# One row of a weight matrix loaded to 32 partitions in six transfers around another matrix's rows, and 29 matrix products fewer, in a decode step bound by its loads

## The chip, the core and the metric

The kernel runs on one NeuronCore of one Trainium2 chip. A core has a matrix engine (TensorE, PE in the profile; its weight loads are shown as PEld), a vector engine (VectorE, DVE), a scalar engine (ScalarE, ACT), GpSimd (POOL) and SyncE (SP), and 16 DMA engines that bring data from HBM into the core's on-chip memory of 128 partitions. DMAs are issued from a queue of SP or ACT. The metric is the device time of one execution in microseconds (us); lower is better.

## The reference, cut to what matters

```python
# B = 2, D = 576, H = 32 heads, Sk = 4096, Dh = 128, F = 4608; all float32
g = sigmoid((x * gate_w).sum(-1, keepdims=True))
q = (x @ wq).reshape(B, 1, H, Dh).transpose(0, 2, 1, 3)
p = softmax(einsum("bhqd,bhkd->bhqk", q, k_cache) * Dh ** -0.5)
a = einsum("bhqk,bhkd->bhqd", p, v_cache).transpose(0, 2, 1, 3).reshape(B, 1, H * Dh) @ wo
b = gelu(x @ w1 + b1) @ w2 + b2
out = g * a + (1 - g) * b
```

One token for each of two sequences: attention over a cache of 4096 keys and values, and a dense layer pair beside it, mixed by a gate. Each weight and each cache entry is read once, 308.6 MB in all.

## The kernel before

**Loads.** All large loads go out on SP's queue in one fixed order: wq, w1, then 16 pairs of a tile of k_cache and a tile of v_cache (each tile is four heads of one sequence, 128 partitions x 16384 floats), then `LAST`: w2 and wo. They land in `ring`, which has three slots of 16384 floats in each partition. A slot is loaded again when the engine that reads it is done, so SP waits for that engine before it issues the load; SP works in order. Each DMA also has one of eight completion semaphores in turn, so it waits until the DMA eight places ahead of it has landed where that isn't known yet.

**w2 and wo as rows.** w2 has 4608 rows of 576; partition p holds its rows 36p to 36p+35, so "row r of w2" in the kernel is a slab of one row from each of the 128 partitions, 36 slabs in all (`NF`). wo is held in the same way as 32 slabs. The list `LAST` (line 66) groups the slabs into the last three ring slots and, within a slot, into transfers. In `load_last` (line 144) each entry is one DMA over 128 partitions, with two exceptions: 384 of the 576 columns of w2's row 35 are left out of the transfer of rows 28 to 35 and go as entry `wx` to 16 partitions, 8 pieces of 384 floats in each, by four DMAs of 4 partitions (line 156); and wo's row 31 goes in three parts (288, 144 and 144 columns).

**What is done with them.** `acc_mm` (line 364) multiplies one slab of w2 (with `hg`, the gated hidden layer) or of wo (with `oP`, the attention result) into the accumulator `acc`, as two products of 288 columns. `mlp_out(lo, hi)` does it for w2's slabs, `wo_out` for wo's, and `mlp_x` for the 384 columns in 16 partitions, with `hx`, a copy of the last column of `hg` spread over 16 partitions by eight small products (line 417). From wo's row `FOLD` = 23 on, `last_out` (line 449) uses another accumulator, `res`, with four products of 144 columns for each row (`part`). ACT meanwhile copies `acc` (line 452), and after row `FOLD` + 3 four products with `fold` add that copy into `res`. Then come the products of rows up to 31, four small copies, and the store of the result.

**The start.** x and gate_w are turned by ten small products (`xps`, line 271): four slabs for w1, the remainder as two, and four slabs again for wq, since the two matrices' rows lie on the partitions differently. Five products (line 280) form the gate's sum `zps`.

**Order of PE's work at the end** (lines 610 to 630): `mlp_out(0, 14)`, the last values tile, `mlp_out(14, 20)` around the attention result's normalisation, `mlp_out(20, 24)`, `mlp_x`, `mlp_out(24, 36)`, `wo_out(0, 23)`, `last_out`. PE works through its products in this order.

Of the kernel before, what the change touches and what calls it, by code (L numbers as in the profile page):

```python
# [12 lines left out]
P = 128  # L13
# [6 lines left out]
def kernel(  # L20
# [47 lines left out]
        (("w2", 28, 36), ("wx", 0, 1), ("wo", 0, 15)),  # L68
        (("wo", 15, 23), ("wo", 23, 27), ("wo", 27, 30), ("wo", 30, 31), ("wo", 31, 32)),
    )  # L70
    FOLD = 23
# [37 lines left out]
    def load_w(w, rows, c):  # L109
        if c < len(rows):  # L110
            n = rows[c] * w.shape[1]
            lo = sum(rows[:c]) * P
            src = w[lo:lo + rows[c] * P].rearrange("(p r) n -> p (r n)", r=rows[c])
        else:
            n = w.shape[1] // 2
            src = w[NX * P:].rearrange("q (e n) -> (q e) n", e=2)
# [18 lines left out]
    XE, XC, XW = 4, 4, 384  # L135
    XL = D - XW
    XP = XE * XC
    XS = P // XP
    srcx2 = w2.rearrange("(e c s r) n -> c r e s n", e=XE, c=XC, s=XS)[:, NF - 1, :, :, XL:]

    def length(w, a, z):
        return XS * XW if w == "wx" else (z - a) * D - (XW if (w, z) == ("w2", NF) else 0)

    def load_last(m):
# [5 lines left out]
        for w, a, z in LAST[m]:  # L150
            if w == "wx":
                xt = t[:XP, o:o + XS * XW]
                rows[w] = xt.rearrange("p (s n) -> p s n", s=XS)
                o += XS * XW
                for c in range(XC):
                    nc.sync.dma_start(xt[c::XC].rearrange("e (s n) -> e s n", s=XS), srcx2[c])
                continue
            if (w, z) == ("w2", NF):
                nc.sync.dma_start(t[:, o:o + length(w, a, z)], srcs[w][:, a * D:z * D - XW])
                for r in range(a, z):  # L160
                    rows[w, r] = t[:, o + (r - a) * D:o + min((r - a + 1) * D, length(w, a, z))]
# [101 lines left out]
    def x_rows(rows):  # L263
        ends = [sum(rows[:c]) * P for c in range(len(rows) + 1)]
        return [xg[:, lo + r:hi:n] for n, lo, hi in zip(rows, ends, ends[1:]) for r in range(n)]

    srcx = x_rows(ROWS["w1"]) + [xe[:, 0], xe[:, 1]] + x_rows(ROWS["wq"])
# [11 lines left out]
    for c in range(NX + 1):  # L279
        nc.tensor.matmul(zps, gT[:, c:c + 1].to_broadcast([P, P]), xT[:, c, :B], start=(c == 0), stop=(c == NX))  # L280
# [8 lines left out]
    def proj(w, ts, banks, width):  # L289
        full = NG * len(banks) * width  # L290
        for c, n in enumerate(ROWS[w] + (1,)):
            last = c == len(ROWS[w])
            for r in range(n):
                k = sum(ROWS[w][:c]) + r
                for m, ps in enumerate(banks):
                    for j in range(NG):
# [4 lines left out]
                        else:  # L301
                            o += r * full
                            lhs = xT[:, k if w == "w1" else NX + 2 + k]
# [112 lines left out]
    for s in range(XS):  # L416
        nc.tensor.matmul(
            hxps[:, s], ident.rearrange("p (q s) -> p s q", s=XS)[:, s], hg[:, NF - 1], start=True, stop=True
        )
# [239 lines left out]
```

## Time and profile before

| | |
|---|---|
| median of 3 runs | 721.73 us (721.68 to 721.9) |
| profiled execution, first to last instruction (span) | 719.7 us |
| median less span: what lies around the instructions | 2.0 us |
| busy: DVE, PE, POOL, ACT | 71%, 31%, 20%, 6% |
| DMA engines busy over the span, SP's queue | 99.2% |
| moved | 308.83 MB, 429 GB/s |

The profiled execution's own device time is not listed apart from its span; the span and the 2.0 us around it together are taken as the 721.73 us of the runs. "L371" is line 371 of the kernel before. In a product's row the count is twice that of the products, as each float32 product is two passes on PE. In a timeline, the time in square brackets is how long the engine sat idle ahead of the row, and what ended that. In rows of windows the columns are: stretch, its length, busy time and count of instructions of each engine, the granted clock of TensorE (1.00 is full), the share of the 16 DMA engines' time spent on packets, and GB/s.

### The profile page before, as it was taken

To read this page: it belongs to the slowest core of one execution; us is meant where nothing else is said; L and a number is where in the kernel's file an instruction comes from. 1 tells how busy PE (TensorE), PEld (TensorE's weight loads), DVE (VectorE), ACT (ScalarE), POOL (GpSimd) and SP (SyncE) were. 2 spreads that over 40 slices of the span, in tenths; PEclk is the share of its full clock that TensorE was granted. 3 is DMA by queue.
4 is the path that set the end of the run, shared out by engine and by line. 5 is a ranking of instruction groups with operands and counts; after the bars stand their busy time and mean duration, and the time that the engine had idled before them with its cause. 6 is when DMAs were issued, how large, how long until landed. Compare 5 with 4: busy or idle time off the path is not lost.

```text
span 719.7 us, 3913 instructions
## 1 busy us (share of the span) xinstructions
PE 223.4 (31%) x1663; PEld 66.1 (9%) x1663; DVE 512.0 (71%) x137; ACT 40.0 (6%) x156; POOL 145.0 (20%) x35
## 2 busy tenths in 40 slices
PE   0675022040514050404133140405060503214198
PEld 0321000010101010101000010101010100000024
DVE  0004969779695969596969879696959695988910
ACT  0110010100001010101010100001010101010000
POOL 2000130404050403022040404040403122040400
PEclk9967557565757575655756575757565665657588
DMA  9999999999999999999999999999999999999997
GB/s 408 412 443 434 426 444 419 455 416 455 416 444 428 426 441 430 438 430 444 430 434 426 441 430 437 431 433 437 437 434 441 423 431 437 430 441 431 420 424 308
DMA packets 7126, 308.83 MB, mean 429 GB/s; under 512 B 810, under 2 KB 1342, under 8 KB 1604
## 3 DMA queue, kind: packets, MB, share of 16 engines
q1 hardware_dynamic: 7060, 308.55, 99.2%
q8 instruction: 13, 0.21, 0.1%
q14 instruction: 5, 0.04, 0.0%
q10 hardware_dynamic: 48, 0.03, 0.0%
HBM read 308.57 MB, written 0.00 MB: 429 GB/s over the span
## 4 chain that ended last, share of the span: by engine, by line
DMA 45%; DVE 35%; PE 17%; ACT 1%; issue 1%; ACTq 0%; POOL 0%; DVEq 0%; POOLq 0%
DMA ring<-in_A_k_cache_dram 39%; DVE ring L512 19%; PE av L551 10%; DVE s L517 10%; DVE s L518 5%; DMA ring<-in_B_w_dram 4%; PE acc L371 3%; DMA ring<-in_gate_w_dram 3%; PE oall L568 2%; PE qps L304 1%; DVE avs L562 1%; PE res L463 0%; ACT p L537 0%; DVE m L522 0%; PE zps L280 0%
## 5 line engine op out<-in xcount | busy, mean ns | idle before, releaser
L512 DVE TENSOR_TENSOR ring<-ring,q 128x16384 f32<-128x16384 f32 x16 | 275.6, 17225 | 110.1 <-DMA ring<-in_A_k_cache_dram 110.1
L516 POOL TENSOR_TENSOR ring<-ring 128x3968 f32<-128x3968 f32 x16 | 137.0, 8565 | 491.3 <-DVE ring L512 491.3
L551 PE MATMUL av<-ring,p 128*32 128x512 f32 x1024 | 141.6, 715 | 167.6 <-ACT p L537 167.6
L517 DVE TENSOR_REDUCE s<-ring 128x66 f32<-128x8448 f32 x16 | 143.2, 8953 | 1.3
L568 PE MATMUL oall<-avs,pick 128*64 128x512 f32 x16 | 14.8, 1028 | 195.1 <-DVE avs L562 167.7
L518 DVE TENSOR_REDUCE s<-ring 128x62 f32<-128x3968 f32 x16 | 68.4, 4277 | 0.1
L551 PEld LDWEIGHTS av<-ring,p 128*32 128x32 f32 x1024 | 36.0, 129 | 278.8 <-issue 220.6
L537 ACT ACTIVATE p<-s,bs 32x128 f32<-32x128 f32 x64 | 25.5, 398 | 479.9 <-DVE bs L531 478.7
L352 PE MATMUL qb<-qm,spread 64*128 64x512 f32 x8 | 8.3, 1138 | 71.4 <-POOL qm L348 71.4
L395 DVE TENSOR_TENSOR ring<-hps,ring 128x384 f32<-128x384 f32 x3 | 1.7, 559 | 32.2 <-PE hps L304 32.0
L371 PE MATMUL acc<-ring,hg 128*2 128x288 f32 (+1 forms) x142 | 14.4, 561 | 25.3 <-DMA ring<-in_B_w_dram 25.3
L568 PEld LDWEIGHTS oall<-avs,pick 128*64 128x64 f32 x16 | 2.2, 196 | 201.9 <-DVE avs L562 201.9
L284 DVE TENSOR_SCALAR gb<-gb 128x2 f32<-128x2 f32 x1 | 0.2, 169 | 24.4 <-ACT gb L283 24.4
L483 DVE COPY ring<-res 2x144 f32<-2x144 f32 x1 | 0.3, 296 | 19.3 <-PE res L463 19.3
L304 PE MATMUL hps<-ring 128*32 128x384 f32 x120 | 12.8, 596 | 0.0
L562 DVE TENSOR_TENSOR avs<-av,selr 128x512 f32<-128x512 f32 x8 | 5.5, 682 | 10.1 <-PE av L551 10.1
L348 POOL TENSOR_TENSOR qm<-qall,mine 64x512 f32<-64x512 f32 x4 | 4.1, 1035 | 40.3 <-ACT qall L331 40.3
L537 ACT ACTIVATION_READ_ACCUMULATOR p<-s,bs 32x1 f32 x64 | 11.8, 184 | 0.0
L304 PE MATMUL qps<-ring 128*32 128x512 f32 x80 | 10.7, 697 | 0.0
L271 PE MATMUL xps<-ident,ring 3*128 3x3 f32 x10 | 1.5, 254 | 23.8 <-DMA ring<-in_gate_w_dram 22.8
L352 PEld LDWEIGHTS qb<-qm,spread 64*128 64x128 f32 x8 | 2.0, 308 | 74.5 <-POOL qm L348 74.5
L354 ACT COPY q<-qb 128x512 f32<-128x512 f32 x4 | 2.3, 585 | 106.3 <-PE qb L352 106.3
(88 smaller groups left out, 79.5 us busy)
## 6 DMA issues: line engine op xcount, KB each, us to landing
ring<-in_B_w_dram SPq DMA_DIRECT2D x2, 4608.0 KB, 34.3
ring<-in_B_w_dram SPq DMA_DIRECT2D x2, 4032.0 KB, 28.6
ring<-in_A_wo_dram SPq DMA_DIRECT2D x1, 4320.0 KB
ring<-in_A_wo_dram SPq DMA_DIRECT2D x1, 2304.0 KB, 22.4
ring<-in_B_w_dram SPq DMA_DIRECT2D x1, 2112.0 KB
ring<-in_B_w_dram SPq DMA_DIRECT2D x1, 1152.0 KB
ring<-in_A_wo_dram SPq DMA_DIRECT2D x1, 1152.0 KB
ring<-in_A_wq_dram SPq DMA_DIRECT2D x1, 1024.0 KB
```

The costliest lines, as they stand in the source:

```text
L304: nc.tensor.matmul(ps[32 * j:32 * j + 32, :width], lhs, ts[c][:, o:o + width], start=(k == 0), stop=last, skip_group_check=True,)
L348: nc.gpsimd.tensor_mul(t, qall.unsqueeze(1).to_broadcast([NO, NQ, DH]), mine[:, u[0]:u[-1] + 1].unsqueeze(2).to_broadcast([NO, NQ, DH]),)
L352: nc.tensor.matmul(ps, spread, t.rearrange("p u d -> p (u d)"), start=True, stop=True)
L371: nc.tensor.matmul(acc[o:o + m, u - s * DS:v - s * DS], lhsT, rhs[:, u - lo:v - lo], start=start, stop=stop, skip_group_check=True,)
L512: nc.vector.tensor_mul(kt[i], kt[i], qs[i].unsqueeze(1).to_broadcast([P, R, DH]))
L516: nc.gpsimd.tensor_add(t[:, :, :DH2], t[:, :, :DH2], t[:, :, DH2:])
L517: nc.vector.tensor_reduce(st[i][:, HALVED:], kt[i][:, HALVED:], AX.X, ALU.add)
L518: nc.vector.tensor_reduce(st[i][:, :HALVED], t[:, :, :DH2], AX.X, ALU.add)
L537: nc.scalar.activation(p[w, :, e * RB:(e + 1) * RB], st[i][w].rearrange("p (t c) -> p t c", c=RB), AF.Exp, bias=bias[i][w], accum_out=rs[w ...
L551: nc.tensor.matmul(ps[32 * j:32 * j + 32], p[:, 32 * t + EB * (1 - half):32 * t + EB * (1 - half) + 32], vt[i][:, RB * t:RB * (t + 1)].rea ...
L562: nc.vector.tensor_mul(t, avs[i].rearrange("p (r d) -> p r d", d=DH), selr.unsqueeze(2).to_broadcast([P, RB, DH]))
L568: nc.tensor.matmul(oall, pick[:, NO - G - i * G:2 * NO - G - i * G], avs[i].rearrange("p r d -> p (r d)"), start=(i == 0), stop=(i == N // ...
```

## The change

Six edits. (1) w2's rows 28 to 34 go to 128 partitions, and row 35 whole to partitions 0 to 31, four pieces of 576 floats in each, by six DMAs: three of 6 partitions ahead of wo's rows 0 to 14, two of 6 and one of 2 partitions behind them. (2) `mlp_x` is 8 products of 288 columns over 32 partitions, where it was 16 (half of them 96 columns wide) over 16 partitions; `mlp_out` no longer has row 35's remaining product of 192 columns; `hx` takes four products instead of eight. (3) `mlp_x` is done behind `wo_out(0, 15)`. (4) `FOLD` goes from 23 to 27, so rows 23 to 26 of wo take two products each instead of four, and the four fold products stand behind row 29 instead of row 26. (5) Both parts of w1 are laid out on the partitions as wq is, four rows to a partition, so x is turned by six products instead of ten; each partition still reads the same lengths in one piece. (6) `zps` is one product, with a multiplication and a sum on DVE ahead of it, instead of five products. Removed are 4 (transposes), 4 (`zps`), 4 (`hxps`), 8 (`mlp_x`), 1 (row 35) and 8 (rows 23 to 26): 29.

```diff
-        (("w2", 28, 36), ("wx", 0, 1), ("wo", 0, 15)),
+        (("w2", 28, 35), ("wx", 0, 3), ("wo", 0, 15), ("wx", 3, 6)),
...
-    FOLD = 23
+    FOLD = 27
...
-            lo = sum(rows[:c]) * P
-            src = w[lo:lo + rows[c] * P].rearrange("(p r) n -> p (r n)", r=rows[c])
+            lo = sum(rows[:c]) * w.shape[1]
+            src = w[:NX * P].rearrange("(p r) n -> p (r n)", r=NX)[:, lo:lo + n]
...
-    XE, XC, XW = 4, 4, 384
-    XL = D - XW
-    XP = XE * XC
+    XE, XP = 6, 32
     XS = P // XP
-    srcx2 = w2.rearrange("(e c s r) n -> c r e s n", e=XE, c=XC, s=XS)[:, NF - 1, :, :, XL:]
+    XT = 768
+    srcx2 = w2.rearrange("(s q r) n -> q s r n", q=XP, s=XS)[:, :, NF - 1]
...
             if w == "wx":
-                xt = t[:XP, o:o + XS * XW]
-                rows[w] = xt.rearrange("p (s n) -> p s n", s=XS)
-                o += XS * XW
-                for c in range(XC):
-                    nc.sync.dma_start(xt[c::XC].rearrange("e (s n) -> e s n", s=XS), srcx2[c])
-                continue
...
+                if a == 0:
+                    rows[w] = t[:XP, o:o + XS * XT].rearrange("p (s n) -> p s n", s=XS)[:, :, :D]
+                for c in range(a, z):
+                    u, v = c * XE, min((c + 1) * XE, XP)
+                    nc.sync.dma_start(rows[w][u:v], srcx2[u:v])
                 o += length(w, a, z)
                 continue
...
-    srcx = x_rows(ROWS["w1"]) + [xe[:, 0], xe[:, 1]] + x_rows(ROWS["wq"])
+    srcx = [xg[:, r:NX * P:NX] for r in range(NX)] + [xe[:, 0], xe[:, 1]]
...
-    for c in range(NX + 1):
-        nc.tensor.matmul(zps, gT[:, c:c + 1].to_broadcast([P, P]), xT[:, c, :B], start=(c == 0), stop=(c == NX))
+    xz = temp((NX + 1) * B).rearrange("p (b c) -> p b c", b=B)
+    nc.vector.tensor_mul(
+        xz, xT[:, :NX + 1, :B].rearrange("p c b -> p b c"), gT.unsqueeze(1).to_broadcast([P, B, NX + 1])
+    )
+    zs = temp(B)
+    nc.vector.tensor_reduce(zs, xz, AX.X, ALU.add)
+    nc.tensor.matmul(zps, ones.to_broadcast([P, P]), zs, start=True, stop=True)
...
     def mlp_x():
         for s in range(XS):
-            acc_mm(hx[:, s], rows["wx"][:, s], s, lo=XL)
+            acc_mm(hx[:, s], rows["wx"][:, s], s)
...
-            if r == FOLD + 3:
+            if r == FOLD + 2:
...
-    mlp_out(20, 24)
+    mlp_out(20, NF - 1)
+    wo_out(0, 15)
     mlp_x()
-    mlp_out(24, NF)
-    wo_out(0, FOLD)
+    wo_out(15, FOLD)
     last_out()
```

PE's last products stand like this in the kernel before, from the end of `mlp_x` (`hx`) through the last of w2's slabs (`hg`) and wo's (`oP`) to the two accumulators `acc` and `res`:

```order
L371 MATMUL acc<-ring,hx 2x96
L371 MATMUL acc<-ring,hx 2x288
L371 MATMUL acc<-ring,hg 2x288 x22
L371 MATMUL acc<-ring,hg 2x192
L371 MATMUL acc<-ring,oP 2x288 x46
L463 MATMUL res<-ring,oP 2x144 x16
L473 MATMUL res<-ring,fold 2x144 x4
L463 MATMUL res<-ring,oP 2x144 x18
L487 MATMUL res<-ring,oP 2x72 x4
```

And in the changed kernel, from the product that turns the attention result (`op_t`) on:

```order
L436 MATMUL op_t<-ring 128x64
L368 MATMUL acc<-ring,hg 2x288 x30
L368 MATMUL acc<-ring,oP 2x288 x30
L368 MATMUL acc<-ring,hx 2x288 x8
L368 MATMUL acc<-ring,oP 2x288 x24
L458 MATMUL res<-ring,oP 2x144 x12
L468 MATMUL res<-ring,fold 2x144 x4
L458 MATMUL res<-ring,oP 2x144 x6
L482 MATMUL res<-ring,oP 2x72 x4
```

The 30 products of wo's rows 0 to 14 now stand ahead of `mlp_x` and right behind w2's slabs, and behind the fold products only 10 products are left, where there were 22.

SP's queue, with what each DMA waits for (a name that begins with DMAHW is a completion semaphore of an earlier DMA), before, from w2's rows 28 to 35 on:

```order
L159 DMA ring<-in_B_w_dram 128x4224 [waits DMAHW4_49,DVE_49]
L156 DMA ring<-in_B_w_dram 4x8x384 x4
L167 DMA ring<-in_A_wo_dram 128x8640 [waits DMAHW5_49]
L167 DMA ring<-in_A_wo_dram 128x4608 [waits DMAHW6_49,PE_49]
L167 DMA ring<-in_A_wo_dram 128x2304 [waits DMAHW7_49,PE_49]
L167 DMA ring<-in_A_wo_dram 128x1728 [waits DMAHW0_49,PE_49]
L167 DMA ring<-in_A_wo_dram 128x576 [waits DMAHW1_49,PE_49]
L167 DMA ring<-in_A_wo_dram 128x288 [waits DMAHW2_49,PE_49]
```

And in the changed kernel:

```order
L163 DMA ring<-in_B_w_dram 128x4032 [waits DMAHW4_49,DVE_49]
L157 DMA ring<-in_B_w_dram 6x4x576 x3
L163 DMA ring<-in_A_wo_dram 128x8640
L157 DMA ring<-in_B_w_dram 6x4x576 [waits DMAHW5_49]
L157 DMA ring<-in_B_w_dram 6x4x576 [waits DMAHW6_49]
L157 DMA ring<-in_B_w_dram 2x4x576 [waits DMAHW7_49]
L163 DMA ring<-in_A_wo_dram 128x4608 [waits DMAHW0_49,PE_49]
L163 DMA ring<-in_A_wo_dram 128x2304 [waits DMAHW1_49,PE_49]
L163 DMA ring<-in_A_wo_dram 128x1728 [waits DMAHW2_49,PE_49]
L163 DMA ring<-in_A_wo_dram 128x576 [waits DMAHW3_49,PE_49]
L163 DMA ring<-in_A_wo_dram 128x288 [waits DMAHW4_49,PE_49]
```

There are two DMAs more, so each wo transfer behind them is handed another completion semaphore: rows 15 to 22 now wait for w2's rows 28 to 34, and the first part of row 31 (128x288) for wo's rows 0 to 14 (128x8640).

More of the change, by code (lines that the diff above doesn't have):

```diff
@@ L133 @@
     srcs = {"w2": w2.rearrange("(p r) n -> p (r n)", r=NF), "wo": wo.rearrange("(p r) n -> p (r n)", r=32)}
-    XE, XC, XW = 4, 4, 384
-    XL = D - XW
-    XP = XE * XC
+    XE, XP = 6, 32
     XS = P // XP
-    srcx2 = w2.rearrange("(e c s r) n -> c r e s n", e=XE, c=XC, s=XS)[:, NF - 1, :, :, XL:]
+    XT = 768
+    srcx2 = w2.rearrange("(s q r) n -> q s r n", q=XP, s=XS)[:, :, NF - 1]
     def length(w, a, z):
-        return XS * XW if w == "wx" else (z - a) * D - (XW if (w, z) == ("w2", NF) else 0)
+        if w == "wx":
+            return XS * XT if a == 0 else 0
+        return (z - a) * D
     def load_last(m):
@@ L151, in load_last @@
             if w == "wx":
-                xt = t[:XP, o:o + XS * XW]
-                rows[w] = xt.rearrange("p (s n) -> p s n", s=XS)
-                o += XS * XW
-                for c in range(XC):
-                    nc.sync.dma_start(xt[c::XC].rearrange("e (s n) -> e s n", s=XS), srcx2[c])
-                continue
[L158 to L161, printed above, removed]
+                if a == 0:
[3 more added lines that the diff above has]
+                    nc.sync.dma_start(rows[w][u:v], srcx2[u:v])
                 o += length(w, a, z)
@@ L262 @@
         nc.scalar.copy(xe[:, e, e::2], xg[:, NX * P:])
-    def x_rows(rows):
-        ends = [sum(rows[:c]) * P for c in range(len(rows) + 1)]
-        return [xg[:, lo + r:hi:n] for n, lo, hi in zip(rows, ends, ends[1:]) for r in range(n)]
-    srcx = x_rows(ROWS["w1"]) + [xe[:, 0], xe[:, 1]] + x_rows(ROWS["wq"])
+    srcx = [xg[:, r:NX * P:NX] for r in range(NX)] + [xe[:, 0], xe[:, 1]]
     NXT = len(srcx)
@@ L302, in proj @@
                             o += r * full
-                            lhs = xT[:, k if w == "w1" else NX + 2 + k]
+                            lhs = xT[:, k]
                         nc.tensor.matmul(
@@ L416 @@
     for s in range(XS):
-        nc.tensor.matmul(
-            hxps[:, s], ident.rearrange("p (q s) -> p s q", s=XS)[:, s], hg[:, NF - 1], start=True, stop=True
-        )
+        nc.tensor.matmul(hxps[:, s], ident[:, s * XP:(s + 1) * XP], hg[:, NF - 1], start=True, stop=True)
     hx = cp.tile([XP, XS, B], F32, name="hx")
```

## The prediction

> **What bounds the kernel now.** I read the page first, then the end of the chain of waits, the timeline there, and windows of the DMA share. The page says that the loads fill the whole span:
>
> ```profile
> span 719.7 us, 3913 instructions
> DMA packets 7126, 308.83 MB, mean 429 GB/s; under 512 B 810, under 2 KB 1342, under 8 KB 1604
> q1 hardware_dynamic: 7060, 308.55, 99.2%
> q8 instruction: 13, 0.21, 0.1%
> DMA 45%; DVE 35%; PE 17%; ACT 1%; issue 1%; ACTq 0%; POOL 0%; DVEq 0%; POOLq 0%
> ```
>
> SP's queue keeps the 16 DMA engines busy for 99.2% of the span, about 26.8 GB/s each (429 / 16). Work on PE or DVE that is removed while they run gains nothing by itself. The chain, followed back from the end, seems to say something else:
>
> ```profile
> 697.20 16.57 PE acc L371 x173
> 715.34 1.44 PE res L463 x36
> ```
>
> By this PE works without a break from 697 us on, and 29 products fewer would end sooner. The timeline shows why that isn't so:
>
> ```profile
> 714.16 0.40 ACT L452 COPY ring<-acc 128x288 f32<-128x288 f32 x1 [18.91 <-PE acc L371]
> 715.25 0.84 PEld L463 LDWEIGHTS res<-ring,oP 128*2 128x2 f32 x32 [0.23 <-DMA ring<-in_A_wo_dram]
> 716.32 0.10 PEld L463 LDWEIGHTS res<-ring,oP 128*2 128x2 f32 x4 [0.23 <-DMA ring<-in_A_wo_dram]
> 716.55 0.48 PE L487 MATMUL res<-ring,oP 128*2 128x72 f32 x8
> 717.46 0.29 SPq L493 DMA_DIRECT2D out_dram<-ring  x1
> ```
>
> PE had caught up before the end: twice in the last 1.5 us it idles 0.23 us for a transfer of wo, and what follows the last one (products, copies, store) is 3.2 us from 716.55 to 719.7, the same in both kernels. So the end is set by when the slowest DMA engine finishes wo's row 31. The windows show the engines running out one by one:
>
> ```profile
> 713.00:713.50 0.50, 0.50 (x13) 0.19 (x10) 0.00 (x0) 0.00 (x0) 0.00 (x0) 1.00 0.93 366
> 713.50:714.00 0.50, 0.50 (x14) 0.21 (x14) 0.00 (x0) 0.00 (x0) 0.00 (x0) 1.00 0.82 333
> 714.00:714.50 0.50, 0.50 (x22) 0.40 (x22) 0.00 (x0) 0.34 (x1) 0.00 (x0) 1.00 0.67 259
> 714.50:715.00 0.50, 0.50 (x22) 0.40 (x18) 0.00 (x0) 0.07 (x1) 0.00 (x0) 1.00 0.69 259
> 715.00:715.50 0.50, 0.50 (x17) 0.24 (x15) 0.00 (x0) 0.00 (x0) 0.00 (x0) 1.00 0.62 218
> 715.50:716.00 0.50, 0.50 (x27) 0.38 (x18) 0.00 (x0) 0.00 (x0) 0.00 (x0) 1.00 0.48 159
> 716.00:716.40 0.40, 0.40 (x18) 0.17 (x12) 0.00 (x0) 0.00 (x0) 0.00 (x0) 1.00 0.25 76
> 716.40:718.20 1.80, 0.63 (x14) 0.20 (x11) 0.60 (x2) 0.55 (x2) 0.00 (x0) 1.00 0.00 0
> ```
>
> The last but one column falls from 0.93 to nothing between 713 and 716.4. Summed, (0.93 + 0.82 + 0.67 + 0.69 + 0.62 + 0.48) x 0.5 + 0.25 x 0.4 = 2.2 us for each engine if it were shared evenly, so with even engines the last byte would land at 715.2 instead of 716.4. That 1.2 us is the most that a better spread of the bytes can bring.
>
> **The change part by part.** First the loads, which decide.
>
> ```profile
> ring<-in_B_w_dram SPq DMA_DIRECT2D x1, 2112.0 KB
> ring<-in_B_w_dram SPq DMA_DIRECT2D x4, 48.0 KB
> DMA packets 111, 0.52 MB, mean 404 GB/s; under 512 B 13, under 2 KB 97, under 8 KB 97
> DMA packets 63, 0.03 MB, mean 44 GB/s; under 512 B 10, under 2 KB 63, under 8 KB 63
> q1 hardware_dynamic: 63, 0.03, 14.5%
> ```
>
> The last three are the counts of packets in the windows 692.3 to 693.6 (the four transfers of 48 KB) and 716.0 to 716.7 (the last part of row 31, 576 bytes a packet). In the second, 53 data packets took 14.5% of 16 engines for 0.7 us, 1.62 us or 31 ns each; 576 bytes at 26.8 GB/s are 21 ns, so a packet costs some 9 ns besides its bytes: an estimate of 66 ns for 1536 bytes and 95 ns for 2304. In the first window 97 - 13 = 84 packets of 1536 bytes went in 1.3 us, 84 x 66 / 1300 = 4.3 engines' worth: a transfer of 4 partitions ran on 4 engines, the same four each time, not on 16. These four carried 32 packets, 2.1 us, that the other twelve did not.
>
> Now: w2's large transfer loses 2112 - 7 x 288 = 96 KB, 0.23 us on every engine. If 6 partitions run on 6 engines, four packets each, and always on the first ones, two engines get 6 x 4 = 24 packets of 2304 bytes (2.28 us), two 20 (1.90 us), and two engines that had none get 20 (1.90 us). Against before: engines 0 and 1 -0.23 + 2.28 - 2.1 = -0.05 us, 2 and 3 -0.43, 4 and 5 +1.67, the other ten -0.23. In all it is the same 308.8 MB. Whether the end moves hangs on which engines are last. By the windows about eight are busy from 715.5 to 716 (0.48 x 16) and four in the last 0.4 us. Four of the eight are likely the ones with 2.1 us more. What made the other four late I read from the packets themselves, strung together by time, which no view prints as rows: the 13 instruction loads of the page's q8 row, 16 KB each, go in turn to eight engines, none of them among the four; the engines that took two such loads are the other late ones, and the four engines with neither kind are done first, where the share falls from 0.93 to 0.67. So the last landing moves by -0.05 us (if engine 0 or 1 is last) to -0.23 us (a plain one). I take -0.1 us. Engines 4 and 5 cost nothing if they finished before 714.7; I take them for two of the four early ones, since instruction loads seem to keep to one half of the engines and the small transfers to the other.
>
> The Trainium skill (DMA: Bandwidth & Descriptors, "Why a DMA increments its semaphore by 16 and not by 1") says that a DMA from SP is spread over the largest number up to 16 that divides the slowest dimension of both its sides, on the lowest-numbered engines. The trace's 4.3 agrees for 4 partitions; no run here shows 6. By that rule it is six engines, the first two taking all six transfers, which is the sum above; with the packets spread over all 16 instead, each engine would get 128 x 95 / 16 ns = 0.76 us, so the four would end 1.6 us earlier, but the plain late ones, and with them the kernel, 0.5 us later.
>
> SP's queue:
>
> ```profile
> 685.27 11.73 SPq L167 DMA_DIRECT2D ring<-in_A_wo_dram x8
> SPq L167 <- DMA ring<-in_B_w_dram: 5.9, 2, 4.6
> ```
>
> Before, all of wo was issued from 685.27 to 697.00, with 5.9 us of waiting for w2 transfers. Now there are two issues more, and rows 15 to 22 wait for w2's rows 28 to 34; the first part of row 31 waits for wo's rows 0 to 14 and stands in line behind everything else. Those rows land at about 704.4: counted back from 716.35 at 26.8 GB/s, an engine's share of 9 + 8 rows (17 x 18 KB = 313 KB, 11.7 us, and small packets). So SP's last three loads go out near 705 instead of 697. The engines reach row 31 only at 712.5 (the share is still above 0.9 then). Cover 7.5 us, cost nothing; without the cover, row 31 would land that much later.
>
> The start:
>
> ```profile
> 24.36 0.87 PE L271 MATMUL xps<-ident,ring 3*128 3x3 f32 x6 [0.94 <-ACT ring L262]
> 25.71 2.26 PE L280 MATMUL zps<-ring 128*128 128x2 f32 x10 [0.48 <-ACT ring L276]
> 36.96 0.33 SPq L130 DMA_DIRECT2D ring<-in_A_k_cache_dram  x1
> 30.00:40.00 10.00, 8.60 (x72) 2.07 (x64) 0.00 (x0) 1.17 (x2) 0.00 (x0) 1.00 1.02 437
> ```
>
> Four transposes fewer save 4 x 0.15 = 0.6 us (0.87 / 6), four `zps` products 4/5 of 2.26 = 1.8 us, and DVE's two new steps give some 0.5 us back, so PE is about 1.9 us early and the first k tile is issued at 35 instead of 37. But the engines are full there (share 1.02): hidden, 0. w1's rows lie farther apart in HBM with the same length in one piece; w2's pieces lie apart as well and load at the full rate (454 GB/s in the window from 680.33, quoted below), so 0; a 1% slower w1 (9 of 308 MB, some 22 us) would be 0.2 us and is in the range. `hxps` (four fewer) runs beside the first key tiles: 0.
>
> PE's tail:
>
> ```profile
> 653.02:656.43 3.41, 1.93 (x20) 0.36 (x12) 3.41 (x1) 0.00 (x0) 0.00 (x0) 1.00 1.00 428
> 680.33:683.74 3.41, 3.41 (x32) 1.03 (x28) 1.96 (x4) 1.18 (x5) 0.00 (x0) 0.50 1.05 454
> 693.98:697.39 3.41, 1.90 (x22) 0.80 (x24) 1.88 (x8) 0.41 (x1) 0.00 (x0) 1.00 0.97 418
> 697.39:700.81 3.42, 3.42 (x38) 1.18 (x32) 0.07 (x1) 0.00 (x0) 0.00 (x0) 0.50 1.13 487
> 700.81:704.22 3.41, 3.41 (x24) 0.81 (x24) 0.00 (x0) 0.00 (x0) 0.00 (x0) 0.50 0.84 360
> 704.22:707.63 3.41, 3.41 (x32) 1.04 (x27) 0.00 (x0) 0.00 (x0) 0.00 (x0) 0.50 1.00 427
> 707.63:711.05 3.42, 3.42 (x63) 2.44 (x59) 0.00 (x0) 0.00 (x0) 0.00 (x0) 1.00 0.99 413
> L371 PE MATMUL acc<-ring,oP 128*2 128x288 f32 x92 | 6.5, 406 | 0.0
> 703.32 0.15 PEld L371 LDWEIGHTS acc<-ring,hg 128*2 128x2 f32 x4 [0.33 <-issue]
> ```
>
> I chose windows at the times (the trace steps the clock every 3.4 us) where the granted clock changes. A window full of 128-row products raises it (680.33), a half-empty one drops it at times (693.98, 1.90 of 3.41 busy) and at times not (653.02, 1.93), and `mlp_x`, with 16 rows, kept it at 0.50 through two full windows (697.39 and 700.81). A product of 288 columns costs 0.24 us at 0.50 (four loads, two products, in 0.48 us) and 0.14 at 1.00 (6.5 / 46). In the changed kernel w2's 30 products come first, so the clock should rise at 700.81 and they end near 702.8: 15 at 0.24, 15 at 0.14. The rest up to `last_out` is 62 products, 8.7 us, so PE alone would be done at 711.5, where it was at 714: 2.5 us less. It then waits for each transfer: about 1.6 us for rows 0 to 14 (704.4), less for the others. The fold products now stand behind rows 27 to 29: eight passes by 0.84 / 32, 0.21 us, put behind a transfer that lands late, but ahead of them PE idles 0.23 us for row 31 (716.32), which covers it just so. ACT's copy of `acc` (0.40 us) can start when row 26 is done, over 1 us ahead of the fold: hidden. Sum on the path: loads -0.1, all else 0: 721.73 - 0.1 = 721.6 us.
>
> **The rivals.**
> PE as the bound. If in runs without a profile PE is later than here, the chain's reading holds and up to the 2.5 us come off: 719.2 us. Against it stand the two waits of 0.23 us; by the profiled run no more than the loads allow can come. It decides if PE idled nowhere behind 715.
> The clock falls at the end. PE now has pauses (702.8 to 704.4, and some 0.5 to 1 us ahead of each later transfer), and if a window is as empty as 693.98 the last 44 passes run at half rate: 44 x 0.026 = 1.1 us more, and some 0.2 us in the last eight: 723.0. Against it: 653.02, as empty, kept the clock, and between 704.4 and 714 PE is mostly busy. The Trainium skill (TensorE: Matmul & The Clock Gate, "What's actually happening") has the clock fall only after an idle window of about 3.4 us that runs free of the program; by that no pause here is long enough, yet the row 693.98 was half busy and fell, so I give the measurement the word.
> The slower side: the two newly loaded engines are late ones. Then the end is theirs: +1.67, less up to 0.23 if they weren't the very last: 723.3 us. It decides once one of them finished behind 714.7 in the trace before; by the windows about four such engines are there besides the four already loaded, and no record names an engine's number, so drawn blindly it would be likely. The split between instruction loads and small transfers speaks against it.
> The change doesn't spread as meant: six partitions run on 2 or 3 engines. On 2, the first two get 64 packets each, 6.1 us instead of 2.1, so -0.23 + 4.0 = +3.8 us: 725.5; on 3, 44 packets or 4.2 us, +1.9: 723.6.
>
> **How the numbers follow.** Forecast (loads -0.05 to -0.23, tail covered) 0.65, 721.4 to 721.8 with its own uncertainty; PE bound 0.08 (faster); clock fall 0.10 (723.0, +0.18%, just inside 0.2%); newly loaded engines late 0.12 (+0.22%, slower); fewer engines 0.05 (slower). A difference of 0.2%, 1.4 us, is about what a measurement of this kernel can tell from none. Faster 0.08, same 0.75, slower 0.17. For 8 in 10 the range takes the forecast and the clock's case and a part of the late engines: 720.7 (the 1.2 us of an even spread, nearly) to 723.1.
>
> **What would show it.** Right: the DMA share still falls to nothing between 713 and 716.4, about 0.1 us earlier; PE idles ahead of wo's rows 0 to 14 and of each later transfer; the clock is 1.00 from about 701 and `mlp_x` takes about 1.1 us instead of 4.0. Wrong: the share's fall ends near 718 with two engines left (late engines) or later (few engines); a clock of 0.50 behind 711; a gap in the DMA share near 705 to 713 (SP's waits).

## The result, and the profile after

The changed kernel takes 725.07 us (725.0 to 725.43, five runs), the kernel before 721.74 us beside it (721.68 to 722.19, five runs): the ratio is 1.0046 (1.0033 to 1.0058), 3.3 us slower, where 721.6 us was forecast. The page of the changed kernel, its span, packets and SP's queue:

```profile
span 723.2 us, 3811 instructions
DMA packets 7141, 308.82 MB, mean 427 GB/s; under 512 B 826, under 2 KB 1230, under 8 KB 1620
q1 hardware_dynamic: 7076, 308.55, 99.0%
```

The same bytes, with the engines as full as before, took 3.5 us longer. The end of the chain of waits says by whom:

```profile
695.96 22.78 DMA ring<-in_A_wo_dram
718.78 0.92 PE res L458 x24
```

PE no longer closes the chain from 697 us on; wo's loads do, until 718.78. The DMA view of the 2 us from 704 to 706, while three of the small transfers are under way, of the kernel before:

```profile
DMA packets 54, 0.88 MB, mean 442 GB/s; under 512 B 6, under 2 KB 6, under 8 KB 6
q1 hardware_dynamic: 54, 0.88, 103.1%
```

and of the changed kernel:

```profile
DMA packets 66, 0.54 MB, mean 271 GB/s; under 512 B 13, under 2 KB 13, under 8 KB 41
q1 hardware_dynamic: 66, 0.54, 104.6%
```

In both the queue keeps 16 engines fully busy (103 and 105%; a packet is counted where it begins), but now they move 0.54 MB instead of 0.88. There are 41 - 13 = 28 packets of 2304 bytes among them; they can't account for it by their own time (28 x 95 ns is 2.7 of 32 engine-us). The other packets are slow. Read one by one from the trace's records, which no view prints as rows, the packets of 34560 bytes that take 1.28 us alone took up to 2.0 us here, those of 18432 bytes 0.73 us in the middle and up to 1.4 instead of 0.69, and those of 2304 bytes up to 0.29 us instead of 0.093: 31 engine-us (microseconds summed over the engines) more than undisturbed, 1.9 us for each of the 16, all but a few tenths of it while row 35's transfers fly. Strung together by time, the records give 16 engines, and slow packets stand in every one of them. In the kernel before there is only about 1 engine-us of that, beside instruction loads.

The end of the loads, in windows (the last columns are the clock, the DMA share, GB/s):

```profile
713.50:714.00 0.50, 0.50 (x8) 0.10 (x8) 0.00 (x0) 0.00 (x0) 0.00 (x0) 1.00 0.97 401
716.00:716.50 0.50, 0.50 (x16) 0.23 (x12) 0.00 (x0) 0.00 (x0) 0.00 (x0) 1.00 0.59 217
717.00:717.50 0.50, 0.50 (x16) 0.23 (x11) 0.00 (x0) 0.00 (x0) 0.00 (x0) 1.00 0.53 183
717.50:718.00 0.50, 0.50 (x12) 0.00 (x1) 0.00 (x0) 0.00 (x0) 0.00 (x0) 1.00 0.31 107
718.00:719.00 1.00, 0.28 (x12) 0.20 (x12) 0.00 (x0) 0.40 (x1) 0.00 (x0) 1.00 0.13 49
719.00:719.90 0.90, 0.90 (x38) 0.77 (x32) 0.00 (x0) 0.00 (x0) 0.00 (x0) 1.00 0.06 21
```

The fall to nothing begins 1 us later and ends at 719.84 (the last packet's record), where it ended at 716.35. Behind 718 there are two engines (0.13 x 16), behind 719 one. The prediction's own measure splits the 3.5 us: take the share from 711 to the last landing, and ask when the last byte would have landed on even engines. One row of the kernel before:

```profile
711.00:716.40 5.40, 5.40 (x120) 3.38 (x114) 0.00 (x0) 0.40 (x1) 0.00 (x0) 1.00 0.78 305
```

and one of the changed kernel:

```profile
711.00:719.90 8.90, 8.18 (x138) 3.35 (x134) 0.00 (x0) 0.40 (x1) 0.00 (x0) 0.93 0.66 264
```

711 + 0.78 x 5.4 = 715.2 before, 711 + 0.66 x 8.9 = 716.9 after. So the even end moved by 1.7 us (all engines later), and the distance from it to the last landing grew from 1.2 to 3.0 us (some engines later still). The first is what the experiments settle; this row is used for each of them.

PE's order of events in the changed kernel, from the timeline, and windows between the steps of its own clock (the column before the DMA share), which are not at the times of the kernel before:

```profile
697.63 5.74 PE L368 MATMUL acc<-ring,hg 128*2 128x288 f32 x60
707.69 6.27 PE L368 MATMUL acc<-ring,oP 128*2 128x288 f32 x60 [4.33 <-DMA ring<-in_A_wo_dram]
713.89 1.15 PE L368 MATMUL acc<-ring,hx 32*2 32x288 f32 x16
714.97 3.09 PE L368 MATMUL acc<-ring,oP 128*2 128x288 f32 x48
718.78 0.92 PE L458 MATMUL res<-ring,oP 128*2 128x144 f32 x24 [0.72 <-DMA ring<-in_A_wo_dram]
```

```profile
698.57:701.99 3.42, 3.42 (x34) 1.20 (x30) 0.00 (x0) 0.00 (x0) 0.00 (x0) 0.50 0.98 425
701.99:705.40 3.41, 1.38 (x20) 0.39 (x12) 0.00 (x0) 0.00 (x0) 0.00 (x0) 1.00 0.96 315
705.40:708.81 3.41, 1.12 (x12) 0.43 (x16) 0.00 (x0) 0.00 (x0) 0.00 (x0) 0.50 0.94 337
708.81:712.23 3.42, 3.42 (x36) 1.03 (x28) 0.00 (x0) 0.00 (x0) 0.00 (x0) 0.50 0.98 418
712.23:715.64 3.41, 3.41 (x52) 1.08 (x48) 0.00 (x0) 0.00 (x0) 0.00 (x0) 1.00 0.95 387
```

PE waits 4.33 us for wo's rows 0 to 14, the clock falls at 705.40, 2.0 us into that wait, and most of the 60 passes behind it run at half rate. Still PE is idle for 0.72 us ahead of 718.78: the loads set the end, PE is next in line by less than a microsecond.

### The profile page after: what moved, and what is told of

It reads as the page before. It is cut to its first block, busy times and chain, and to the rows that moved or that the text cites. A ratio compares the mean times of both kernels' runs of the same rounds, so it can differ in the third digit from the quotient of the medians.

```text
span 723.2 us, 3811 instructions
## 1 busy us (share of the span) xinstructions
PE 214.8 (30%) x1609; PEld 60.7 (8%) x1609; DVE 512.3 (71%) x139; ACT 40.0 (6%) x156; POOL 144.9 (20%) x35
## 4 chain that ended last, share of the span: by engine, by line
DMA 50%; DVE 35%; PE 13%; ACT 0%; issue 0%; SPq 0%; DVEq 0%; ACTq 0%
DMA ring<-in_A_k_cache_dram 39%; DVE ring L507 19%; PE av L546 10%; DVE s L512 10%; DMA ring<-in_B_w_dram 9%; DVE s L513 5%; DMA ring<-in_A_wo_dram 3%; PE oall L563 2%; PE acc L368 1%; DVE avs L557 1%; ACT p L532 0%; DVE m L517 0%; DVE mt L522 0%; DVE bs L526 0%; PE res L458 0%
## 5 line engine op out<-in xcount | busy, mean ns | idle before, releaser
L546 PE MATMUL av<-ring,p 128*32 128x512 f32 x1024 | 139.2, 705 | 172.8 <-ACT p L532 172.8
L368 PE MATMUL acc<-ring,hg 128*2 128x288 f32 x140 | 13.5, 543 | 24.3 <-DMA ring<-in_B_w_dram 24.3
L368 PE MATMUL acc<-ring,oP 128*2 128x288 f32 x108 | 9.4, 502 | 4.3 <-DMA ring<-in_A_wo_dram 4.3
```

Source lines behind the costliest of these rows:

```text
L368: nc.tensor.matmul(acc[o:o + m, u - s * DS:v - s * DS], lhsT, rhs[:, u - lo:v - lo], start=start, stop=stop, skip_group_check=True,)
L546: nc.tensor.matmul(ps[32 * j:32 * j + 32], p[:, 32 * t + EB * (1 - half):32 * t + EB * (1 - half) + 32], vt[i][:, RB * t:RB * (t + 1)].rea ...
```

## The experiments

All times are medians with the ratio to the kernel before, run beside each (721.68 to 721.75 us). "Slow packets" are sums over the packet records as above, in engine-us.

**Which part of the change.** Theory A: the loads of row 35 carry the whole cost. Theory B: the other edits carry a part. First the changed kernel with the loads, `hx` and `mlp_x` of before:

```diff
-        (("w2", 28, 35), ("wx", 0, 3), ("wo", 0, 15), ("wx", 3, 6)),
+        (("w2", 28, 36), ("wx", 0, 1), ("wo", 0, 15)),
...
-    mlp_out(20, NF - 1)
-    wo_out(0, 15)
+    mlp_out(20, 24)
     mlp_x()
-    wo_out(15, FOLD)
+    mlp_out(24, NF)
+    wo_out(0, FOLD)
```

> All of the change but its loads and mlp_x: row 35 is loaded and multiplied as in the kernel before, 384 columns on 16 partitions in four transfers. Theory A (the loads of row 35 in six transfers cost it all): as before, 721.7 us. Theory B (the fold products behind row 29, FOLD = 27, w1's layout or the start cost it): 724 to 725 us.

Measured: 721.89 us (721.79 to 722.17), ratio 1.0001 (0.9992 to 1.0011). Then the kernel before with those parts of the changed one, the same diff turned round:

> The kernel before with the change's loads of row 35, its mlp_x and the place of mlp_x alone. Theory A: 725 us as the changed kernel, with the DMA rate between 703.5 and 708 us near 306 GB/s instead of 414. Theory B: 721.5 to 722 us.

Measured: 724.87 us (724.03 to 725.19), ratio 1.0039 (1.0024 to 1.0054), with 33 engine-us of slow packets. Its window 711 on, after that of the run before:

```profile
711.00:716.80 5.80, 5.61 (x109) 3.52 (x104) 0.00 (x0) 0.40 (x1) 0.00 (x0) 1.00 0.72 286
```

```profile
711.00:719.10 8.10, 7.32 (x146) 3.25 (x140) 0.00 (x0) 0.40 (x1) 0.00 (x0) 1.00 0.77 304
```

Even ends: 715.2 without row 35's new loads, 717.2 with them. Theory A holds; `FOLD`, w1's layout and `zps` cost and bring nothing that can be measured (0.2 us between the medians), and B falls.

**Where in the memory.** The large transfers run over all 128 partitions. No record names an engine's number; what follows takes engine e for the one that carries the e-th partition of a small transfer. Then the kernel before placed its four transfers so that engine e wrote only partitions 4e to 4e + 3 (`xt[c::XC]`: partition c of each group of four), and six partitions side by side on six engines put engine 1 in partition 1, engine 5 in partition 5, and so on. Theory W: packets written into partitions that belong to another engine's part of the large transfers hold all engines up. Theory R: the cost is on the side that is read. First each transfer's destination set 5 partitions apart, with `hx` spread to match and its products put ahead of the loads of the last slot (these edits are left out here and below):

```diff
-                    nc.sync.dma_start(rows[w][u:v], srcx2[u:v])
+                    nc.sync.dma_start(rows[w][c:30:5] if c < 5 else rows[w][u:v], srcx2[u:v])
...
```

> The changed kernel, with each transfer of 6 written to partitions five apart instead of side by side; the rows read by each transfer are the same (x's copy of the hidden layer is permuted to fit). Theory W (neighbouring partitions share a way into the memory, so six engines that write side by side hold each other and the others up): no packets slower than their size, 723.0 to 723.6 us if the load of six engines is all that is left, 721.6 if it is hidden. Theory R (the pattern of rows read from HBM): unchanged, 725 us.

Measured: 729.85 us, ratio 1.0113 (1.0098 to 1.0128). The slow packets are half of what they were, 14 engine-us, but the time is longer for another reason, which ACT's timeline names:

```profile
708.02 0.41 ACT L623 COPY ring<-ident 128x128 f32<-128x128 f32 x1 [23.59 <-DMA ring<-in_B_w_dram]
```

The copy `turn` (of the identity matrix, for turning the attention result) lies in the same slot, and with a destination in steps it waits for the last small transfer, where in the changed kernel it began at 690.46; PE then waits 12.9 us for `turn`. So the run says nothing by its time. The source in steps of 5 instead, the destination as in the changed kernel:

```diff
-                    nc.sync.dma_start(rows[w][u:v], srcx2[u:v])
+                    nc.sync.dma_start(rows[w][u:v], srcx2[c:30:5] if c < 5 else srcx2[u:v])
...
```

> The changed kernel, with the six engines of each transfer reading rows five times as far apart in w2 (415 KB instead of 83 KB) and writing partitions side by side as in the changed kernel. Theory R (rows 83 KB apart, read by six engines at once, collide in HBM): the slow stretch goes, 721.6 to 723.6 us. Theory W (the writing side): unchanged, 725 us.

Measured: 724.91 us (724.21 to 725.02), ratio 1.0039 (1.0024 to 1.0054), slow packets 32 engine-us. From 704 to 706, by the DMA view:

```profile
DMA packets 70, 0.52 MB, mean 259 GB/s; under 512 B 13, under 2 KB 13, under 8 KB 47
q1 hardware_dynamic: 70, 0.52, 107.0%
```

The same picture as in the changed kernel: R falls. The first of the two again, with `turn` in a tile of its own (theory L in this text and the next: what costs is the load on engines that carried no small packets before; theory X: packets of 2304 bytes, or 32 destination partitions, are slow anyhow):

```diff
-    turn = late(P)
+    turn = qp.tile([P, NQ, DH], F32, tag="q", name="turn")[:, 0]
```

> The changed kernel with each transfer of 6 written to partitions five apart, and the copy for the turn of the attention result in a tile of its own, since in the run before it ACT waited until 708.0 us for row 35's last transfer before it made that copy, and PE with it. Theory W: between, since five apart keeps the six engines of one transfer out of each other's groups but not out of those of the large transfers: 723 to 724 us. Theory L: 723.3 to 725 us.

Measured: 724.84 us (723.7 to 725.86), ratio 1.0043 (1.0029 to 1.0056). That is above W's range and within L's. In steps of 5 no two engines of one transfer write the same group of four, but for the last one of 2 partitions; still 22 of the 32 partitions lie in another engine's group (26 in the changed kernel), and 16 engine-us of slow packets are left: 4 beside the first three transfers, where 9 of 18 partitions are foreign, 13 beside the last three, where 13 of 14 are. The window from 711 on:

```profile
711.00:720.70 9.70, 8.32 (x141) 3.37 (x137) 0.00 (x0) 0.40 (x1) 0.00 (x0) 0.96 0.53 212
```

The even end, 716.1, lies between 715.2 and 716.9, as W would have it; but one engine landed its last packet at 720.65, why isn't shown, so the time isn't lower. By its time this run is inconclusive. The next pair isn't: eight partitions for each of four transfers, so that eight engines carry 16 packets each, all ahead of wo's rows 0 to 14. Once every engine writes its own four partitions:

```diff
-        (("w2", 28, 35), ("wx", 0, 3), ("wo", 0, 15), ("wx", 3, 6)),
+        (("w2", 28, 35), ("wx", 0, 4), ("wo", 0, 15)),
...
-    XE, XP = 6, 32
+    XE, XP = 8, 32
...
-                    nc.sync.dma_start(rows[w][u:v], srcx2[u:v])
+                    nc.sync.dma_start(rows[w][c::4], srcx2[c::4])
```

(`turn` has its own tile here too.)

> The changed kernel with row 35 in four transfers of 8 partitions, all ahead of wo's rows 0 to 14: transfer c takes partitions c, c+4, ... c+28, so that engine e writes only partitions 4e to 4e+3 (taking engine e for the e-th partition of a transfer). The copy that ACT makes for the turn of the attention result stands in a tile of its own. Theory W (neighbouring groups of four partitions share a way in, and an engine holds the others up when it writes into a group that is not its own): no packet slower than its size, 721.4 to 721.8 us. Theory L (what costs is the load on engines that had none, 16 packets or 1.5 us on each of eight): 723 us. Theory X (packets of 2304 bytes, or 32 destination partitions, are slow anyhow): 724 to 726 us.

And once with the eight partitions side by side (`rows[w][u:v]`, `srcx2[u:v]`), all else the same:

> As the run with partitions c, c+4, ... c+28, but transfer c takes partitions 8c to 8c+7, side by side: the same engines, packets and bytes, and two groups of four partitions that eight engines write at once. Theory W: the slow stretch is back, 1 to 3 us more than that run. Theories L and X: the same time as that run.

Measured: 722.41 us (721.34 to 722.71) and 724.39 us (722.54 to 725.64); ratios 1.0006 (0.9997 to 1.0015) and 1.0033 (1.0022 to 1.0044). In the first no packet is slow but a few beside instruction loads, in the second 30 engine-us are lost. The first is still 0.6 us above W's range: of its 11 runs four took 721.34 to 721.65 us, seven 722.41 to 722.71. Windows of the first, then of the second:

```profile
691.50:696.00 4.50, 3.74 (x41) 1.08 (x29) 1.88 (x5) 0.00 (x0) 0.00 (x0) 1.00 1.06 444
711.00:717.30 6.30, 4.52 (x92) 2.11 (x90) 0.00 (x0) 0.40 (x1) 0.00 (x0) 1.00 0.63 248
```

```profile
691.50:696.00 4.50, 3.52 (x37) 1.09 (x29) 2.07 (x6) 0.00 (x0) 0.00 (x0) 1.00 1.08 322
711.00:719.80 8.80, 8.80 (x128) 3.29 (x124) 0.00 (x0) 0.31 (x1) 0.00 (x0) 0.82 0.67 269
```

The same packets, on as many engines, at the same place in the queue: 444 against 322 GB/s with the engines as full, even ends 715.0 and 716.9, and 2.0 us between the medians. Theory W holds, as far as the placing goes. How the loss reaches the end differs from the changed kernel: in the second run's profiled execution, the slowest of its seven, PE waits 5.97 us for wo's rows 0 to 14, its clock falls there, and behind that wait it closes the chain of waits:

```profile
708.57 10.86 PE acc L368 x124
```

That span ends 4.1 us behind the last landing, the first run's 3.4 us, so some 0.7 us of it is PE's own work, late and at half rate. The Trainium skill (DMA: Bandwidth & Descriptors, "The descriptor swizzle") says that in a transfer over 128 partitions engine 8(p >> 6) + ((p >> 2) & 7) writes partition p, so that each engine writes one port of that memory; SBUF — State Buffer, "Door 1: The DMA port swizzle (why `[64,N]` ≈ `[32,N]`)" has four neighbouring partitions on a port. The pair agrees with it: it is the placing by groups of four that is fast. That the ports are what is contended is an inference: the runs vary the placing (and with it the rows read, which the run with the source in steps showed not to matter), and why engines that by this rule write none of partitions 0 to 31 are slowed too isn't explained by it. Nor do the runs part writing into a foreign group from several engines crowding in one group; the run in steps of 5 shows that the first costs without the second.

The same test on the kernel before, its four transfers written side by side:

```diff
-    srcx2 = w2.rearrange("(e c s r) n -> c r e s n", e=XE, c=XC, s=XS)[:, NF - 1, :, :, XL:]
+    srcx2 = w2.rearrange("(c e s r) n -> c r e s n", e=XE, c=XC, s=XS)[:, NF - 1, :, :, XL:]
-                    nc.sync.dma_start(xt[c::XC].rearrange("e (s n) -> e s n", s=XS), srcx2[c])
+                    nc.sync.dma_start(xt[c * XE:(c + 1) * XE].rearrange("e (s n) -> e s n", s=XS), srcx2[c])
```

(Each partition holds the same rows of w2 as before; which four rows a transfer reads changes with the placing.)

> The kernel before with its four transfers of 4 partitions written side by side (4c to 4c+3) instead of four apart (c, c+4, c+8, c+12); the same four engines, packets and bytes. Theory W: slower than before by about 1 us (72 packets less in flight than in the changed kernel, whose first three transfers lost 0.5 us on every engine and the last three 1.2 us). Theories L and X: 721.7 us.

Measured: 722.8 us (722.7 to 723.4), ratio 1.0016 (1.0007 to 1.0025), 6 engine-us of slow packets.

```profile
711.00:718.30 7.30, 6.11 (x128) 3.56 (x122) 0.00 (x0) 0.40 (x1) 0.00 (x0) 1.00 0.69 272
```

Even end 716.0. So placing the four transfers side by side costs the kernel before 1.1 us, as W expected. The slow packets are 0.4 us of that for each engine; what the rest is isn't shown. Nor does the loss go by the number of misplaced packets: 96 of 128 here lost 6 engine-us, 104 of 128 in the changed kernel 31.

**What a load on few engines costs without slow packets.** No small transfer at all, row 35 whole over 128 partitions:

```diff
-        (("w2", 28, 35), ("wx", 0, 3), ("wo", 0, 15), ("wx", 3, 6)),
+        (("w2", 28, 36), ("wo", 0, 15)),
...
```

> The changed kernel with no small transfers at all: rows 28 to 35 of w2 go in one transfer over 128 partitions, wo's rows 0 to 14 behind it, and 72 products of 288 columns use them all. Theory W (the cost of the change is packets of an engine that land outside the partitions it writes in the large transfers): none do, so no packet of 34560 bytes should take over 1.4 us and the window 703.5 to 708 should move 410 GB/s or more. Every engine carries the same here but for the instruction loads, 0.23 us more than before, and the four engines with the small transfers 1.9 us less; the end is set by the engines with two instruction loads: 721.7 + 0.2 = 721.9 us (721.5 to 722.4). Rival (the engines' load decides and the kernel before gains by its small transfers on free engines): the same 0.2 us, so this run tells nothing between these two; a rival by which the edits outside the loads cost something together with whole rows would give 724 to 725.

Measured: 722.08 us (722.0 to 722.36), ratio 1.0006 (0.9997 to 1.0014). No packet is slow but beside instruction loads. The kernel before gains 0.4 us by its small transfers, if anything (the interval is -0.2 to 1.0 us). Then the transfers of before issued twice, the second set to the same place:

> The kernel before, with its four transfers of 4 partitions each issued twice, the same data to the same place: 32 packets of 1536 bytes more on each of four engines (2.1 us each), each in the partitions its engine writes anyway. It prices load on four engines without packets outside their partitions. Engine-load theory: the four end later by 2.1 us; as they were among the last eight (between 715.5 and 716.4), the end moves by 1.6 to 2.1 us: 723.3 to 723.8. If the load of some engines is made up elsewhere (the queue evens it out): 721.7 to 722.3. The packets of 34560 and 18432 bytes should keep their 1.28 and 0.69 us in either case, by theory W.

Measured: 727.17 us (726.59 to 728.16). SP's waits and the window show why this doesn't price the load:

```profile
SPq L156 <- DMA ring<-in_B_w_dram: 7.9, 1, 7.9
```

```profile
691.50:696.00 4.50, 4.33 (x44) 1.19 (x36) 1.38 (x4) 0.00 (x0) 0.00 (x0) 1.00 0.37 137
```

SP waited for the first set before it wrote there again, wo's loads stood behind it, and the engines ran dry (share 0.37). What the text expected of the packets failed too: 16 engine-us of them are slow, though every engine wrote its own partitions. About half of that is in the first 13 packets of 34560 bytes behind the gap, which began together from 697.03 on and took 1.4 to 2.3 us. The kernel before has the same where its loads begin: its first 16 packets of 65536 bytes, one on each engine, took 2.5 to 3.4 us, the next ones 2.42. So engines that began together had slow packets here with no misplaced one beside them; in the changed kernel there is no such gap while row 35 flies (share 1.10 from 691.5 to 696, and 0.94 or more in the windows between the clock's steps). With the second set to a place of its own behind wo's rows 0 to 9:

```diff
-        (("w2", 28, 36), ("wx", 0, 1), ("wo", 0, 15)),
-        (("wo", 15, 23), ("wo", 23, 27), ("wo", 27, 30), ("wo", 30, 31), ("wo", 31, 32)),
+        (("w2", 28, 36), ("wx", 0, 1), ("wo", 0, 10), ("wx", 1, 2)),
+        (("wo", 10, 23), ("wo", 23, 27), ("wo", 27, 30), ("wo", 30, 31), ("wo", 31, 32)),
...
-                rows[w] = xt.rearrange("p (s n) -> p s n", s=XS)
+                rows[w] = rows.get(w, xt.rearrange("p (s n) -> p s n", s=XS))
```

> The kernel before with its four transfers of 4 partitions issued a second time to a place of their own, behind wo's rows 0 to 9 (rows 10 to 22 are one transfer then), so that SP need not wait for the first set: 32 packets of 1536 bytes, 2.1 us, more on each of the same four engines, all in the partitions these engines write anyway. It prices load on a few engines alone. The data read twice isn't used. Engine-load theory (the spread failed as well): the four were among the last and end 2.1 us later: 723.3 to 723.8 us, two thirds of what the change cost. If the lag of some engines is small or made up: 721.7 to 722.3, and the cost of the change is then the slow packets alone. No packet of 34560 or 18432 bytes is slow in either case, and the window 691.5 to 696 moves 440 GB/s or more.

Measured: 728.54 us (728.08 to 729.83). The copy `turn` again, and PE behind it:

```profile
703.68 0.41 ACT L620 COPY ring<-ident 128x128 f32<-128x128 f32 x1 [18.89 <-DMA ring<-in_B_w_dram]
704.15 0.69 PE L441 MATMUL op_t<-ring 128*128 128x64 f32 x2 [7.08 <-ACT ring L620]
```

The time is PE's; the last landing is at 718.63, and hardly a packet was slow. With `turn` in its own tile:

> The run before this one again (the four transfers of 4 partitions a second time, to a place of their own behind wo's rows 0 to 9), with the copy `turn` in a tile of its own, so that ACT's copy no longer waits for the second set (it waited until 703.68 there, and PE 7.1 us for it). In that run the last packet landed at 718.63, where it was 716.35 before, with no slow packets. Engine-load theory: the four loaded engines set the end again at about 718.6, so 721.7 + 2.3 = 724.0 us (723.3 to 724.3). If the late landing there came from the late PE and not from the engines: 721.7 to 722.3.

Measured: 723.79 us (723.56 to 724.84), ratio 1.003 (1.0018 to 1.0043), last landing 718.31, no slow packets. While the second set flies, from 700 to 702:

```profile
DMA packets 115, 0.90 MB, mean 448 GB/s; under 512 B 13, under 2 KB 88, under 8 KB 88
q1 hardware_dynamic: 115, 0.90, 106.0%
```

88 - 13 = 75 small packets in 2 us, and 448 GB/s: in an engine's own partitions they cost their own time and no more. And that time counts in full: 2.1 us more on four engines moved the last landing by 2.0 us and the median by 2.0 us. (The profiled execution, 724.7 us, was one of the two slowest of six; in it PE was still at work without a pause when the last packet landed, so some of its own time is PE's.)

**The place in the queue.** The changed kernel with all six transfers ahead of wo's rows 0 to 14:

```diff
-        (("w2", 28, 35), ("wx", 0, 3), ("wo", 0, 15), ("wx", 3, 6)),
+        (("w2", 28, 35), ("wx", 0, 6), ("wo", 0, 15)),
```

> The changed kernel with all six transfers of row 35 ahead of wo's rows 0 to 14, where three stood ahead and three behind. The partitions written and the engines' loads are the same. Theory W: the slow packets stay (25 to 35 engine-us in all) but in one stretch, where w2's rows 28 to 34 and wo's rows 0 to 14 run, and the window 703.5 to 708 is back at 400 GB/s or more: 724 to 725.5 us. If the place behind rows 0 to 14 is what costs (six SP issues late, or the slow stretch close to the end): 722 to 723.

Measured: 724.3 us (723.95 to 725.48), ratio 1.004 (1.0027 to 1.0053), 25 engine-us of slow packets.

```profile
691.50:696.00 4.50, 4.19 (x44) 1.19 (x36) 1.52 (x4) 0.00 (x0) 0.00 (x0) 1.00 1.01 292
703.50:708.00 4.50, 0.70 (x8) 0.29 (x12) 0.00 (x0) 0.00 (x0) 0.00 (x0) 0.78 0.92 396
711.00:718.60 7.60, 7.60 (x116) 3.00 (x112) 0.00 (x0) 0.36 (x1) 0.00 (x0) 0.88 0.74 295
```

The loss moves with the transfers: 292 GB/s in the early window, 396 (just short of the 400 expected) in the late one, and the even end is 716.6. The median is 0.8 us less than the changed kernel's; the intervals of the two ratios overlap. So the place isn't what costs in the main; whether it adds something isn't shown.

## Why the prediction was wrong, point by point

**The step that failed: the sum over the loads.** "In all it is the same 308.8 MB" counted each engine's packets at the durations of the kernel before, 95 ns for a small one and nothing lost by the others. Nothing in the records speaks against the count (24, 20 and 20 packets on six engines), though none names an engine, and the price was right where nothing disturbs (93 ns when each engine writes its own partitions). What was left out is that where an engine writes sets the speed of all: 31 engine-us of slow packets, the even end 1.7 us later instead of unchanged. The term of -0.1 us measured +3.3 (+3.1 with the loads and `mlp_x` alone). The diff showed it: `xt[c::XC]` became `rows[w][u:v]`, and the working passed over the placing.

**Engines 4 and 5 "cost nothing".** The distance from the even end to the last landing grew by 1.8 us, near the +1.67 that the rival gave to the newly loaded engines, and its sign, a fall that ends with two engines left, stands in the windows (0.13 behind 718). A pure load counts in full, as the doubled transfers showed (+2.0 for 2.1). But with 1.9 us of slow packets spread unevenly over the same engines, the trace doesn't tell how much of the 1.8 us is load: that stays open. The rival alone gave 723.3 and would not have reached 725.

**SP's queue** was right in its price of 0, though the last loads went out at 709, behind a wait of 10.1 us, and not near 705; the DMA share stayed at 0.94 or more up to 715.6 (windows between the clock's steps, above):

```profile
694.74 14.44 SPq L163 DMA_DIRECT2D ring<-in_A_wo_dram  x7
SPq L163 <- DMA ring<-in_A_wo_dram: 10.1, 1, 10.1
```

**The start** was right in its price of 0, by the run without the new loads. PE's products for q begin and end 2 us earlier, as worked out; yet the first k tile went out only 0.8 us earlier, since SP then waited for a transfer of w1 until 36.03. The kernel before:

```profile
27.91 10.70 PE L304 MATMUL qps<-ring 128*32 128x512 f32 x80
```

and the changed kernel, with the piece of its chain of waits that ends at 36.03:

```profile
26.02 10.52 PE L301 MATMUL qps<-ring 128*32 128x512 f32 x80
1.65 34.38 DMA ring<-in_B_w_dram
36.12 0.33 SPq L130 DMA_DIRECT2D ring<-in_A_k_cache_dram  x1
```

**PE's tail.** The 30 products of w2 ended at 703.4, 0.6 us behind what was worked out (702.8), and `mlp_x` took 1.15 us (1.1). Rows 0 to 14 came at 707.7 instead of 704.4; the loads without slow packets bring them at 705.9 (eight engines, own partitions) and 705.5 (no small transfers), so a good 1 us was a wrong estimate and the rest is the slow packets. The clock fell in that wait and not at the end as the rival had it (the sign that it gave, 0.50 behind 711, stood until 712.23); it cost 6.27 - 4.05 = 2.2 us on the 60 passes against the run with own partitions, all covered by 0.72 us:

```profile
705.93 4.05 PE L368 MATMUL acc<-ring,oP 128*2 128x288 f32 x60 [3.04 <-DMA ring<-in_A_wo_dram]
```

So the gain on PE, 29 products fewer, was real and worth nothing, as forecast. "PE as the bound" didn't occur, and "fewer engines" hardly: by the records up to six small packets are under way at once.

**What no version reached.** None of the kernels tried beats the kernel before by more than can be measured; the nearest, eight engines with their own partitions, has runs from 721.34 to 722.71. In its profiled execution, one of the slower ones, about one engine is busy from 716 on; by the records strung together it is one that took an instruction load.

## What to carry to other kernels

When the DMA engines are the bound, count a small transfer by the engines that it runs on and also by the partitions that each of these writes: place partition k of the transfer in the group of partitions that engine k writes in the large transfers around it, or, as here, it can slow all 16. To see it, compare GB/s at the same DMA share (271 against 442 at 104%), since the busy share hides it. A destination in steps can make later work in the same buffer wait for it, so look at who else lives in the slot.

## What the runs showed of the hardware that was not expected

- Packets of 2304 bytes written side by side by six or eight engines held up packets of other engines and other transfers: 34560 bytes took up to 2.6 us instead of 1.28 (six transfers ahead of wo's rows 0 to 14), and 16 busy engines moved 259 to 322 GB/s instead of 440. With each engine in its own group of four partitions the packets took 93 ns and disturbed nothing.
- The side that is read doesn't matter here: the same source rows in steps of 5 gave 259 GB/s, side by side 271.
- Packets were also slow, with no misplaced ones beside them, where all engines began together: 2.5 to 3.4 us instead of 2.42 at the start of the kernel before.
- PE's clock fell in or just behind waits of 4.2 to 6.0 us, was kept through the one of 3.04 us above and lost in one of 2.86 us, in the last of the runs with doubled transfers (36 passes in 3.96 us, 0.11 us each, are half rate; 60 in 4.05 full):

```profile
712.31 3.96 PE L371 MATMUL acc<-ring,oP 128*2 128x288 f32 x36 [2.86 <-DMA ring<-in_A_wo_dram]
708.76:712.17 3.41, 0.69 (x10) 0.09 (x2) 0.00 (x0) 0.00 (x0) 0.00 (x0) 1.00 0.91 381
```

So the length of the wait alone doesn't decide it. Between the steps of each trace's own clock, the stretches that ended in a fall in these waits had PE busy for 0 to 1.4 of 3.41 us (0.69 in the row above, 1.38 in the changed kernel), and stretches with 1.72 and 2.07 us kept the clock in the run with own partitions; in the kernel before 1.90 fell and 1.93 did not. The Trainium skill (TensorE: Matmul & The Clock Gate, "What's actually happening") ties the fall to an idle window of about 3.4 us that runs free of the program; the waits of 5.44 us (all transfers ahead) and 5.97 us (eight engines side by side), each with one such stretch wholly idle, agree with that, the falls behind 1.38 and 0.69 us of work don't.
